# Denominators' epsilon on ScalarE, first loads interleaved, and new engine orders in a linear-attention and GEGLU block

## The chip, the cores and the metric

The kernel runs on one core of a Trainium2 chip. The metric is the device time of one execution in microseconds; the time before is the median of six runs. One further thing is read: one profiled execution, whose trace gives every instruction's start and length on each engine.

## The reference

A transformer block on x of 2048 rows and 448 columns, in bf16: layer norm, linear attention with 16 heads of 28, a residual; layer norm, a gated GELU feed-forward of width 1792, a residual.

```python
q, k, v = qkv[0], qkv[1], qkv[2]
phi = lambda t: jnp.where(t > 0, t + 1, jnp.exp(t)) + 1e-6
pq, pk = phi(q), phi(k)
kv = jnp.einsum("bhsd,bhse->bhde", pk, v)
z = jnp.einsum("bhsd->bhd", pk)
num = jnp.einsum("bhqd,bhde->bhqe", pq, kv)
den = jnp.einsum("bhqd,bhd->bhq", pq, z)[..., None] + 1e-6
o = num / den                     # then @ wo, and h = x + o @ wo
h2 = h + (gelu(hn @ w_gate) * (hn @ w_up)) @ w_down      # hn = layernorm(h)
```

## The kernel before

The rows are 16 tiles of 128. Every piece of work is a named task on one engine, written with what it reads and writes; the engines' orders are five lists of task numbers (`ORDERS`), and each engine runs its list strictly in order, waiting on semaphores where a task's inputs come from elsewhere. So an instruction that waits holds up everything behind it in its list. The number after the underscore is a tile, or a job of the feed-forward.

Stage A, for each tile t: `bnst1_t` and `bnag1_t` on VectorE (statistics, L347 and L348), `ln1_t` and `rstd1_t` on ScalarE (L354, L356: the reciprocal root as exp of -0.5 log). Tiles 0 to 3 are normalised on VectorE (`normD_t`, L369), transposed on TensorE (`tr0_t`, `tr1_t`, L377) and copied out by ScalarE and VectorE (`evxA_t`, `evxD_t`). Tiles 4 to 15 are normalised on GpSimd (`normP_t`, L387) and transposed by DMA from SP's queue (`xT_t`, L389), which stands behind all the first loads. Then TensorE projects `k_t` and `q_t` (L403), four matmuls each; ScalarE and VectorE make phi(k) (`ek_t`, `ck_t`, `pk_t`), and TensorE sums pk against the normalised x and a column of ones into four PSUM banks (`pt4_t`, L422; for the last tile `pt1_15` and `pt3_15`). Q is evacuated by ScalarE twice (`eq_t` exp, `rq_t` relu, L430 and L431) and joined on VectorE (`cq_t`, `aq_t`).

Between the stages the sums are brought to SBUF: `z1`, `z0` (the sum of phi(k), on all partitions), `evpA`, `evpD`; `kv` forms the heads' matrices (L461), `kvm` masks them to the heads' blocks on VectorE (L465), `w2_g` multiplies by Wo and `evwA`, `evwD` copy the result.

Stage B, for tiles in pairs: the product phi(q) z (`t1`, L487, on GpSimd but for tile 0), `dr_t` sums it per head (L490), `de_t` adds epsilon (L492), `rd_t` takes the reciprocal (L493), `pn_t` scales phi(q) by it (L494), all on VectorE. The pair is transposed, the first on TensorE (`tro`, copied by `evo`), the others by DMA (`oT_p`, L509). `out2_t` applies the w2 matrices (L522), `hr_t` adds x (L528), and the second layer norm follows: statistics on VectorE, the root on GpSimd (`negm2`, `vpe2`, `pow2`), `nhP_t` on GpSimd (L557), `wrap_t` on VectorE, `hT_t` a DMA transpose on SP (L560). The first pair goes through ScalarE, VectorE (`nhD_t`, `wr64_t`) and TensorE (`trh_t`, L549; `evhA_0`, `evhD_1`).

The feed-forward runs in chunks of 2, 2, 4, 4 and 4 tiles. A job is one bank of gate and one of up: `gu2_0` to `gu2_13` (28 matmuls of 256 columns) for the first four tiles, `gu4_14` to `gu4_55` (14 of 512) for the rest. Gate and up have two banks each; a job's halves go through ScalarE (`ge0_v`, `ge1_v`, gelu, L622) and VectorE (`hm0_v`, `hm1_v`, times up, L624), and the bank is free after that. `gu2_7` needs `hT_2` and `hT_3`; `gu4_14` needs `hT_4` to `hT_7`; `gu4_28` and `gu4_42` the next four each. `down448_t` multiplies by W_down (L574), `fo448_t` adds the residual (L578), `do_t` stores.

SP's queue carries, in order: the first loads (x tile by tile or in groups, Wk, Wq, Wv, Wo), the `xT` transposes, the gate and up weights, then `oT`, `hT` and stores as listed, with the load of W_down (`dwd`) among them. ScalarE's queue issues two loads at the start, the second of which (the last 64 rows of Wk) waits for a GpSimd memset, and only then its first table load.

Of the kernel before, what the change touches and what calls it, by code (L numbers as in the profile page):

```python
# [6 lines left out]
F32 = mybir.dt.float32  # L7
ALU = mybir.AluOpType
AF = mybir.ActivationFunctionType
# [6 lines left out]
    "28 34 36 45 43 65 75 70 78 52 54 63 61 91 81 69 130 86 74 85 101 113 90 125 105 140 117 152 129 164 144 156"  # L16
    " 176 168 188 203 193 215 180 227 192 242 207 219 231 246 247 257 248 251 288 232 260 292 290 294 296 254 263"
    " 312 269 314 316 317 272 275 266 353 330 334 431 436 441 446 451 456 384 461 503 508 415 466 469 513 518 523"
    " 528 533 575 580 585 590 487 541 595 600 605 610 615 620 625 630 635 640 559 538 672 648 703 645 654 651 719"
    " 724 729 734 739 744 749 754 759 764 769 774 779 784 801 806 811 816 821 826 831 836 841 846 851 856 861 866"  # L20
    " 789 792 795 798 871 874 877 880 883",
    "4 6 27 31 32 40 41 35 44 66 76 49 50 58 59 77 53 96 71 62 97 92 108 93 109 82 80 120 121 135 136 87 79 147 148"
    " 102 114 159 171 160 131 172 198 132 126 141 199 183 222 184 210 211 223 153 165 237 177 238 189 204 194 216"
    " 228 195 243 282 286 285 249 259 250 258 252 234 233 262 253 291 261 255 295 313 315 271 264 265 256 273 274"
    " 324 325 267 326 270 327 276 277 268 331 336 434 432 437 439 444 442 447 449 454 452 459 457 462 464 506 511"
    " 509 504 516 514 519 521 526 524 529 531 536 534 576 578 581 583 588 586 593 591 596 598 603 601 606 608 611"
    " 613 616 618 623 621 626 628 633 631 636 638 643 641 720 722 725 727 732 730 735 737 742 740 747 745 752 750"
    " 755 757 760 762 767 765 770 772 777 775 782 780 787 785 802 804 809 807 812 814 819 817 822 824 827 829 834"
    " 832 839 837 844 842 847 849 854 852 859 857 864 867 869 862",
    "29 30 38 39 33 42 37 46 47 56 48 67 57 94 51 95 60 68 55 106 64 107 133 118 72 119 73 134 83 145 84 157 88 146"  # L30
    " 196 208 89 158 169 103 170 104 115 197 181 116 209 220 127 221 182 128 142 143 339 154 155 300 298 166 235 167"
    " 236 340 178 179 190 301 191 337 205 299 338 217 206 218 229 230 369 244 370 245 284 283 302 287 304 305 308"
    " 306 289 343 402 344 347 309 293 310 307 345 311 346 348 297 349 350 375 318 376 321 319 400 377 320 322 546"
    " 323 403 328 371 332 333 329 372 357 335 401 379 354 358 355 380 359 435 433 381 378 438 356 440 382 445 443"
    " 544 406 448 407 450 364 474 367 410 472 411 408 412 547 453 455 460 409 458 659 475 413 473 657 463 465 385"
    " 388 386 482 389 483 512 387 484 390 688 416 507 419 505 417 420 660 418 478 421 395 398 510 554 690 555 470"
    " 556 517 479 515 426 691 520 429 522 545 527 525 667 485 530 532 480 550 537 535 481 668 658 577 579 551 669"
    " 582 584 467 589 557 663 587 664 689 552 491 553 492 594 592 488 489 694 597 599 490 698 604 602 493 695 607"
    " 609 612 614 696 699 501 617 619 700 701 624 622 670 627 629 498 665 634 632 666 639 637 697 644 542 560 563"
    " 561 642 564 565 562 539 673 676 573 674 675 570 649 704 677 705 678 707 646 706 708 709 721 723 714 683 652"  # L40
    " 726 728 717 733 731 736 738 686 743 741 748 746 655 753 751 756 758 761 763 768 766 771 773 778 776 783 781"
    " 788 786 803 805 810 808 813 815 820 818 823 825 828 830 835 833 840 838 845 843 848 850 855 853 860 858 868"
    " 790 793 863 870 796 865 799 872 875 878 881 884",
    "16 1 18 19 21 22 0 17 23 20 2 24 98 99 110 111 25 122 137 123 138 26 149 150 161 173 162 174 200 212 224 185"
    " 186 201 213 225 239 240 303 341 342 373 374 405 404 361 362 360 366 363 477 549 391 392 393 476 394 397 423"
    " 424 422 662 428 425 548 661 693 692 494 495 496 500 497 567 566 568 572 569 680 679 711 681 710 712 682 716"
    " 713 685",
    "3 5 7 8 9 10 11 12 13 14 15 100 112 124 139 151 163 175 187 202 214 226 241 278 279 280 281 351 352 383 365"
    " 368 414 396 471 399 427 430 486 468 558 671 702 499 502 540 543 574 571 647 718 687 653 684 656 715 650 791"
    " 797 800 873 794 879 876 882 885",  # L50
# [120 lines left out]
def bass_sequential_preLN__linear_attn_block__glu_gated_geglu__prompt_kernel(  # L171
# [14 lines left out]
    SEQ = "K0 K1 Q0 Q1 K2 K3 Q2 K4 K5 K6 Q3 K7 K8 K9 K10 K11 Q4 K12 K13 K14 Q5 K15 Q6 Q7 Q8 Q9 Q10 Q11 Q12 Q13 Q14 Q15"  # L186

    G = _Graph()
    es = ExitStack()
    with es:  # L190
        block = es.enter_context(nc.Block())

        def sb(name, shape, dt):
            return es.enter_context(nc.sbuf_tensor(name, shape, dt))
# [37 lines left out]
        den = sb("den", [128, 4, H, 2], F32)  # L232
# [11 lines left out]
        def bufs(name, n):  # L244
            return [_Buf("%s%d" % (name, i)) for i in range(n)]
# [8 lines left out]
            _Buf(n) for n in ("ident", "ones", "mones", "mtmp", "mask", "eps", "mhalf", "powtmp"))  # L254
        b_st1, b_mv1, b_nm1, b_ln1, b_rs1 = bufs("st1", T), bufs("mv1", T), bufs("nm1", T), bufs("ln1", T), bufs("rs1", T)
# [25 lines left out]
        def dma(q, out_ap, in_ap, w, name, r=(), after=()):  # L281
            t_ = G.add(q, lambda e: e.dma_start(out_ap, in_ap), r=r, w=w, name=name, kind="dma", after=list(after) + last[q])
            last[q] = [t_]
            return t_
# [11 lines left out]
        def dma_x(q, a, b):  # L296
            dma(q, x_sb[:, a:b, :], xv[:, a:b, :], b_x[a:b], "dx%d" % a)
# [4 lines left out]
        dma_x("act", 1, 2)  # L302
        dma_w3("sp", wk_sb, D, b_wk, "dwk")
        tk = dma_w1("act", wk_sb, D, b_wk, "dwk_t")
        dma_w3("sp", wq_sb, 0, b_wq, "dwq")
        dma_w1("sp", wq_sb, 0, b_wq, "dwq_t")
        dma_x("sp", 2, 4)
# [10 lines left out]
        op("pool", lambda e: e.memset(eps_t[:], EPS_LN), [], [b_eps], "eps")  # L318
        op("pool", lambda e: e.memset(mhalf[:], -0.5), [], [b_mhalf], "mhalf")
# [10 lines left out]
        tbl1 = G.add("act", lambda e: e.preload_act_table_set("natural_log_exp_and_others"), name="tbl1", kind="nosync", after=[tk])  # L330
# [147 lines left out]
        def a2_pair(p):  # L478
# [9 lines left out]
            for t in (a, a + 1):  # L488
                n, i = t % 2, t % 4
                op("dve", lambda e, n=n, i=i: e.tensor_reduce(den[:, i, :, 0], t1[:, n, :].rearrange("p (h d) -> p h d", h=H), AX.X, ALU.add),  # L490
                   [b_t1[n]], [b_den[i]], "dr_%d" % t)
                op("dve", lambda e, i=i: e.tensor_scalar(den[:, i, :, 0], den[:, i, :, 0], EPS, None, ALU.add), [b_den[i]], [b_den[i]], "de_%d" % t)  # L492
                op("dve", lambda e, i=i: e.reciprocal(rd[:, i, :], den[:, i, :, 0]), [b_den[i]], [b_rd[i]], "rd_%d" % t)  # L493
# [196 lines left out]
```

## Time and profile before

| what | value |
|---|---|
| median of six runs | 199.15 us (198.57 to 199.94) |
| the profiled execution | 199.94 us |
| its span, first to last instruction | 198.2 us |
| TensorE busy | 187.9 us |
| VectorE busy | 135.8 us |
| ScalarE busy | 74.6 us |
| GpSimd busy | 49.8 us |
| mean granted TensorE clock | 1.0 |

The profiled execution is the slowest of the six runs, 0.79 us above the median; 1.7 us of it lie outside the span. Matmul ends are modelled, so the length of a stage on TensorE is read from the starts of its tasks. "PEld" is TensorE's weight load, which overlaps matmuls.

### The profile page before, as it was taken

How to read it: one execution, taken by the hardware profiler on the slowest of the kernel's cores; microseconds unless marked ns; L12 is line 12 of the kernel's file. 1: busy time of each engine (PE TensorE's matmuls, PEld its weight loads, DVE VectorE, ACT ScalarE, POOL GpSimd, SP SyncE). 2: the span in 40 equal slices, each digit the busy share in tenths (PEclk: the TensorE clock that was granted, in tenths of full speed). 3: DMA queues.
4: the chain of work that ended last, by engine and by line, in shares of the span. 5: the costliest groups of instructions: out<-in, count | busy, mean ns of one | idle time of the engine just before them, and what ended most of it. 6: DMA issues, size and time to landing. Idle time of an engine off the chain costs nothing.

```text
span 198.2 us, 4143 instructions
## 1 busy us (share of the span) xinstructions
PE 187.9 (95%) x1572; PEld 114.0 (58%) x1572; DVE 135.8 (69%) x371; ACT 74.6 (38%) x210; POOL 49.8 (25%) x92
## 2 busy tenths in 40 slices
PE   7998999998899699979999999999999999999994
PEld 7444555644577565854445555545677777645553
DVE  3899978899899989687967787607645544424221
ACT  3795745698933120324133410013344344310000
POOL 6065640440353257513223013370000000000000
PEclk9999999999999999999999999999999999999999
DMA  6994448997907701623200187202630000000112
GB/s 182 370 171 81 91 97 170 222 219 130 315 4 83 120 3 22 139 50 76 46 11 0 24 134 154 55 0 50 134 74 3 0 0 3 0 10 16 46 46 73
DMA packets 35812, 16.98 MB, mean 86 GB/s; under 512 B 27728, under 2 KB 34512, under 8 KB 35792
## 3 DMA queue, kind: packets, MB, share of 16 engines
q1 hardware_dynamic: 35568, 16.55, 37.9%
q8 instruction: 12, 0.20, 0.5%
q10 hardware_dynamic: 224, 0.17, 0.3%
q14 instruction: 8, 0.07, 0.1%
HBM read 8.26 MB, written 1.84 MB: 51 GB/s over the span
## 4 chain that ended last, share of the span: by engine, by line
PE 75%; DVE 12%; DMA 8%; ACT 2%; issue 1%; ACTq 0%; DVEq 0%
PE ps L602 24%; PE ps L574 21%; PE ps L604 13%; PE ps L403 7%; DMA hnT<-hn 5%; PE ps L422 5%; PE ps L522 4%; DMA xnT<-xnn 2%; DVE den L490 2%; DVE den L492 1%; DMA x_sb<-in_A_x_dram 1%; DVE st L347 1%; DVE hh L624 1%; DVE pqn L494 1%; DVE x_sb L528 1%
## 5 line engine op out<-in xcount | busy, mean ns | idle before, releaser
L602 PE MATMUL ps<-hnT,wgu_sb 64*128 64x512 bf16 (+1 forms) x490 | 86.5, 333 | 3.6 <-DMA hnT<-hn 2.9
L604 PE MATMUL ps<-hnT,wgu_sb 64*128 64x512 bf16 (+1 forms) x490 | 86.7, 334 | 0.6 <-DVE hh L624 0.5
L622 ACT ACTIVATE gl<-ps 128x256 bf16<-128x256 f32 x112 | 36.9, 381 | 83.9 <-PE ps L604 76.2
L624 DVE TENSOR_TENSOR hh<-ps,gl 128x256 bf16<-128x256 f32 x112 | 42.8, 417 | 34.0 <-ACT gl L622 33.8
L602 PEld LDWEIGHTS ps<-hnT,wgu_sb 64*128 64x128 bf16 x490 | 45.2, 94 | 20.1 <-ACT gl L622 3.4
L604 PEld LDWEIGHTS ps<-hnT,wgu_sb 64*128 64x128 bf16 x490 | 42.5, 94 | 11.5 <-DVE hh L624 6.5
L574 PE MATMUL ps<-wd_sb,hh 128*128 128x448 bf16 (+1 forms) x238 | 43.4, 341 | 0.0
L574 PEld LDWEIGHTS ps<-wd_sb,hh 128*128 128x128 bf16 x238 | 23.1, 98 | 19.6 <-issue 0.4
L487 POOL TENSOR_TENSOR t<-pq,zbc 128x448 f32<-128x448 bf16 x15 | 16.2, 1090 | 38.7 <-DVE pq L483 25.3
L347 DVE BATCH_NORM_STATS2 st<-x_sb 128x6 f32<-128x448 bf16 x32 | 19.0, 608 | 3.8 <-DMA x_sb<-in_A_x_dram 3.7
L578 DVE TENSOR_TENSOR x_sb<-ps,x_sb 128x448 bf16<-128x448 f32 (+1 forms) x17 | 10.1, 592 | 15.2 <-PE ps L574 15.1
L403 PE MATMUL ps<-wk_sb,xnT 128*128 128x448 bf16 x64 | 14.4, 352 | 0.7 <-DMA xnT<-xnn 0.7
L522 PE MATMUL ps<-w,pqnT 112*128 112x448 bf16 x64 | 13.6, 353 | 0.6 <-DVE mv L348 0.6
L422 PE MATMUL ps<-pk,xnn 128*128 128x448 bf16 x64 | 14.0, 353 | 0.0
L403 PE MATMUL ps<-wq_sb,xnT 128*128 128x448 bf16 x64 | 13.8, 353 | 0.0
L528 DVE TENSOR_TENSOR x_sb<-ps,x_sb 128x448 bf16<-128x448 f32 x16 | 9.6, 615 | 2.3 <-PE ps L522 2.3
L414 ACT ACTIVATE e<-ps 128x448 bf16<-128x448 f32 x16 | 8.7, 544 | 6.3 <-PE ps L403 5.6
L387 POOL TENSOR_SCALAR xnn<-x_sb,nm,rs 128x448 bf16<-128x448 bf16 x12 | 8.8, 736 | 5.6 <-PE ps L422 2.9
L557 POOL TENSOR_SCALAR hn<-x_sb,nm,rs 128x448 bf16<-128x448 bf16 x14 | 10.0, 725 | 0.3
L416 DVE SCALAR_TENSOR_TENSOR pk<-ps,e 128x448 bf16<-128x448 f32 x16 | 9.7, 614 | 0.3 <-DVE e L415 0.2
L403 PEld LDWEIGHTS ps<-wk_sb,xnT 128*128 128x128 bf16 x64 | 6.1, 98 | 6.7 <-ACT rs L356 1.1
L522 PEld LDWEIGHTS ps<-w,pqnT 112*128 112x128 bf16 x64 | 5.7, 97 | 7.3 <-issue 1.3
(67 smaller groups left out, 141.8 us busy)
## 6 DMA issues: line engine op xcount, KB each, us to landing
out_dram<-x_sb SPq DMA_DIRECT2D x15, 112.0 KB, 1.7
wd_sb<-in_B_w_down_dram SPq DMA_DIRECT2D x1, 1568.0 KB, 7.6
x_sb<-in_A_x_dram SPq DMA_DIRECT2D x3, 448.0 KB, 5.4
wgu_sb<-in_B_w_gate_dram SPq DMA_DIRECT2D x1, 896.0 KB, 13.0
wgu_sb<-in_B_w_up_dram SPq DMA_DIRECT2D x1, 896.0 KB, 16.0
wgu_sb<-in_B_w_gate_dram SPq DMA_DIRECT2D x1, 672.0 KB, 5.9
wgu_sb<-in_B_w_up_dram SPq DMA_DIRECT2D x1, 672.0 KB, 8.4
wo_sb<-in_A_wo_dram SPq DMA_DIRECT2D x1, 392.0 KB, 7.3
```

Of the source, the lines that this page charges most:

```text
L347: op("dve", lambda e: e.bn_stats(st[:, t, :], src_ap), [b_src], [b_st[t]], "bnst%s_%d" % (tag, t))
L403: ins = e.matmul(ps[:, bk, 0:D], xnT[:, t, k, :], w[:, k, :], start=(k == 0), stop=(k == 3))
L422: ins = e.matmul(ps[:, BK_PT[c], 0:D], xnn[:, t % XN_R, c * 128:(c + 1) * 128], pk[:, i, :], start=(t == 0), stop=(t == T - 1))
L487: op(eng, lambda e, t=t, n=n: e.tensor_tensor(t1[:, n, :], pq[:, t, :], zbc[:, :], ALU.mult), [b_pq[t]] + b_z, [b_t1[n]], "t1%s_%d" % (eng ...
L522: ins = e.matmul(ps[:, BK_OUT[n], 0:D], pqnT[0:GW, i2, n, g, :], w2[:, g, :], start=(g == 0), stop=(g == NG - 1))
L528: op("dve", lambda e, t=t, bo=bo: e.tensor_tensor(x_sb[:, t, :], ps[:, bo, 0:D], x_sb[:, t, :], ALU.add), [b_ps[bo], b_x[t]], [b_x[t]], "h ...
L574: ins = e.matmul(psO, hh[:, j, (t % HR) * 128:(t % HR + 1) * 128], wd_sb[:, j, c0:c1], start=(j == 0), stop=(j == NJ - 1))
L578: op("dve", lambda e, t=t, psO=psO, c0=c0, c1=c1: e.tensor_tensor(x_sb[:, t, c0:c1], psO, x_sb[:, t, c0:c1], ALU.add), [b_ps[bk], b_x[t]], ...
L602: e.matmul(psG[:, jj * N:(jj + 1) * N], wgu_sb[A_, k, j * 128:(j + 1) * 128], hnT[A_, ka_, c0:c0 + N], start=(k == 0), stop=(k == NK - 1))
L604: ins = e.matmul(psU[:, jj * N:(jj + 1) * N], wgu_sb[B_, k, j * 128:(j + 1) * 128], hnT[B_, kb_, c0:c0 + N], start=(k == 0), stop=(k == NK ...
L622: G.add("act", lambda e, gi=gi, cs_=cs_, psG=psG: e.activation(gl[:, gi, cs_], psG[:, cs_], AF.Gelu_apprx_tanh), r=[b_ps[BK_G[i]]], w=[b_g ...
L624: op("dve", lambda e, dst=dst, srcU=srcU, srcL=srcL: e.tensor_tensor(dst, srcU, srcL, ALU.mult), [b_ps[BK_U[i]], b_glh], [b_ar[j_][t % HR] ...
```

## The change

Three things change. The add of epsilon to the denominators is a ScalarE instruction (an Identity activation whose bias is a column `eps_d`, which GpSimd fills), and `den` loses its unused second column. At the start tile 2 of x is loaded ahead of Wq and tile 3 behind it, and the last 64 rows of Wk are issued by SP behind the rest of Wk, not by ScalarE. The five orders and the order of K and Q (`SEQ`) are new: an order was searched with a model in which DMA transposes take time to issue.

```diff
-    SEQ = "K0 K1 Q0 Q1 K2 K3 Q2 K4 K5 K6 Q3 K7 K8 K9 K10 K11 Q4 K12 K13 K14 Q5 K15 Q6 Q7 ..."
+    SEQ = "Q0 K0 K1 Q1 K2 Q2 K3 K4 K5 Q3 K6 K7 K8 K9 K10 K11 K12 K13 Q4 K14 Q5 K15 Q6 Q7 ..."
...
         dma_x("sp", 0, 1)
-        dma_x("act", 1, 2)
+        tx1 = dma_x("act", 1, 2)
         dma_w3("sp", wk_sb, D, b_wk, "dwk")
-        tk = dma_w1("act", wk_sb, D, b_wk, "dwk_t")
+        dma_w1("sp", wk_sb, D, b_wk, "dwk_t")
+        dma_x("sp", 2, 3)
         dma_w3("sp", wq_sb, 0, b_wq, "dwq")
         dma_w1("sp", wq_sb, 0, b_wq, "dwq_t")
-        dma_x("sp", 2, 4)
+        dma_x("sp", 3, 4)
...
+        op("pool", lambda e: e.memset(eps_d[:], EPS), [], [b_epsd], "epsd")
...
-        tbl1 = G.add("act", ..., name="tbl1", kind="nosync", after=[tk])
+        tbl1 = G.add("act", ..., name="tbl1", kind="nosync", after=[tx1])
...
-                op("dve", lambda e, i=i: e.tensor_scalar(den[:, i, :, 0], den[:, i, :, 0], EPS, None, ALU.add), [b_den[i]], [b_den[i]], "de_%d" % t)
-                op("dve", lambda e, i=i: e.reciprocal(rd[:, i, :], den[:, i, :, 0]), [b_den[i]], [b_rd[i]], "rd_%d" % t)
+                op("act", lambda e, i=i: e.activation(den[:, i, :], den[:, i, :], AF.Identity, bias=eps_d[:, 0:1]), [b_den[i], b_epsd], [b_den[i]], "deA_%d" % t)
+                op("dve", lambda e, i=i: e.reciprocal(rd[:, i, :], den[:, i, :]), [b_den[i]], [b_rd[i]], "rd_%d" % t)
```

TensorE's order around the two stages, before and after (the jobs in a row shortened to a range):

```
before: ... k_12 q_4 k_13 pt4_10 k_14 pt4_11 k_15 pt4_12 pt4_13 pt4_14 pt1_15 pt3_15 q_9 q_6 q_7 kv
        q_5 q_10 w2_1 w2_0 w2_2 w2_3 q_8 q_11 tro_0 q_13 tro_1 out1_0 out1_1 q_14 q_15 q_12
        out2_2 trh_0 trh_1 gu2_0-5 out2_4 gu2_6-8 out2_6 down_0 down_1 gu2_9-13 gu4_14-17 out2_8
        down_3 gu4_18-27 out2_10 down_2 out2_12 down_5 out2_14 down_4 down_7 down_6 gu4_28-55 ...
after:  ... k_12 k_13 q_4 k_14 q_5 k_15 pt4_11 pt4_12 pt4_13 pt4_14 pt1_15 pt3_15 q_7 q_6 kv
        q_8 w2_1 w2_0 q_11 w2_3 q_9 w2_2 tro_0 q_10 tro_1 out1_0 out1_1 q_15 q_12 q_13 q_14
        trh_0 trh_1 out2_2 gu2_0 gu2_1 out2_4 gu2_2-5 out2_6 gu2_6-12 down_1 down_0 out2_8 gu2_13
        gu4_14 gu4_15 down_2 out2_10 gu4_16-19 down_3 out2_12 gu4_20-27 out2_14 down_4 down_5
        down_6 gu4_28-43 down_7 down_8 down_9 down_10 gu4_44-55 ...
```

On VectorE the new order of the first tiles is: statistics of tiles 0 and 1 around `normD_0`, statistics of tile 2, `evxD_0`, `normD_1`, `normD_2`, `evxD_1`. On ScalarE `rstd1_4` stands behind `rq_2`, and the adds stand as `deA_0` to `deA_5` among the evacuations of Q, `deA_7` first behind the GELU table load, the other nine between gelu halves. On SP `dwd` stands behind `oT_1 oT_2 oT_3 hT_3 hT_2`, where it stood behind `oT_1`.

## The prediction

> **What bounds the kernel now.** The page's first part comes first: TensorE is busy for 95% of the span and has the same 1,572 matmuls in any order, so the change can only win or lose TensorE's idle time.
>
> ```profile
> span 198.2 us, 4143 instructions
> ## 1 busy us (share of the span) xinstructions
> PE 187.9 (95%) x1572; PEld 114.0 (58%) x1572; DVE 135.8 (69%) x371; ACT 74.6 (38%) x210; POOL 49.8 (25%) x92
> ```
>
> Then I cut the span where the kind of work changes (busy us of each engine per stretch):
>
> ```profile
> core 0: us, PE busy (x) PEld busy (x) DVE busy (x) ACT busy (x) POOL busy (x), PEclk, DMA share, GB/s
> 6.30:16.60 10.30, 9.57 (x55) 4.36 (x52) 9.81 (x29) 8.41 (x27) 4.66 (x11) 1.00 0.87 232
> 16.60:36.30 19.70, 19.67 (x104) 10.20 (x105) 16.50 (x48) 10.62 (x31) 7.37 (x15) 1.00 0.59 122
> 36.30:53.10 16.80, 15.00 (x105) 8.22 (x105) 16.13 (x45) 14.95 (x35) 5.60 (x5) 1.00 0.97 217
> 53.10:68.10 15.00, 13.03 (x204) 9.98 (x204) 14.54 (x43) 5.73 (x15) 6.40 (x8) 1.00 0.52 84
> 68.10:87.70 19.60, 18.17 (x232) 13.16 (x233) 17.36 (x49) 4.61 (x14) 9.36 (x14) 1.00 0.31 62
> 87.70:195.30 107.60, 107.53 (x830) 63.51 (x830) 58.73 (x154) 27.66 (x84) 13.22 (x23) 1.00 0.20 43
> ```
>
> The reader should see that after 87.7 us TensorE idles for 0.07 us: nothing can be won there. Between 36.3 and 87.7 us VectorE is busy for 48.0 of 51.4 us and TensorE idles for 5.2; there VectorE, and the round trips through it, set the pace. Then the waits (total, times, longest) and two pieces of the chain (start, length):
>
> ```profile
> PEld ps L604 <- DVE hh L624: 6.5, 27, 0.6
> PE ps L602 <- DMA hnT<-hn: 2.9, 2, 1.6
> ```
> ```profile
> 62.98 5.04 DMA hnT<-hn
> 83.16 4.43 DMA hnT<-hn
> ```
>
> The two largest holes are gu2_7 waiting for hT_3 (1.65 us before 68.15) and gu4_14 waiting for hT_7 (1.23 us before 87.73). Many small ones are gate/up jobs waiting until VectorE frees their bank.
>
> **The change, step by step.** I follow the new order engine by engine with durations of the trace, start to next start where instructions stand back to back: a projection 0.757, gu2 1.525, gu4 1.512, out2 1.51, down 2.655 us on TensorE; on VectorE bn_stats, dr, pn, hr 0.53, hm 0.34, aq 0.30, cq and wrap 0.18, rd 0.16; a DMA transpose 1.25 us to issue, 2.5 (xT) to 3.1 us (oT, hT) to land.
>
> *The add of epsilon.* Sixteen instructions leave VectorE, sixteen join ScalarE.
>
> ```profile
> L492 DVE TENSOR_SCALAR den<-den 128x16 f32<-128x16 f32 x16 | 5.0, 313 | 0.0
> L354 ACT ACTIVATE ln<-mv,eps_t 128x1 f32<-128x1 f32 x18 | 5.0, 288 | 2.6 <-DVE mv L348 2.5
> L356 ACT ACTIVATE rs<-ln 128x1 f32<-128x1 f32 x18 | 3.5, 199 | 0.3
> ```
> ```profile
> 39.77 2.10 POOL L487 TENSOR_TENSOR t<-pq,zbc 128x448 f32<-128x448 bf16 x2
> 40.87 1.03 DVE L492 TENSOR_SCALAR den<-den 128x16 f32<-128x16 f32 x1
> ```
>
> The median add took 168 ns; the mean is 313 because some lie under a GpSimd product of L487 and stretch, one to 1.03 us. VectorE is rid of 16 x 0.31 = 5.0 us of busy time, some 3 us of it in the 51 us where it paces. On ScalarE the nearest row is the Ln with a bias pointer: 0.29 us (the Exp without one 0.20), so 16 x 0.29 = 4.6 us. The Trainium skill speaks against this: "ScalarE: Activation LUTs", in its rules for kernel authors, sends an add to VectorE and budgets about 0.3 us for each ACTIVATE with a bias pointer. By that rule ScalarE pays 4.8 us to relieve VectorE of 16 x 0.17 = 2.7 at the undisturbed price, a loss. The rows let me choose the other way: the price on VectorE was 5.0, and ScalarE has room where ten of the adds go (5.73 of 15.0 and 4.61 of 19.6 us busy). The other six fall where it has 1.85 us free in 16.8 (14.95 busy); that cover is thin, and is the first rival. Each rd now waits for two hops: dr's end, then 0.05 + 0.29 + 0.05 us. Behind it on VectorE stand pn and the hm's, for which TensorE waits. In the new order 0.3 to 2 us of other VectorE work stands between most dr and their rd, so I cost the hop at nothing; uncovered it is up to 0.4 us x 12 tiles.
>
> *The front.* The last 64 rows of Wk move from ScalarE's queue to SP's, tile 2 of x goes ahead of Wq, tile 3 behind it: 13 loads on SP instead of 11, the same bytes. Wk landed at 4.68; the 56 KB behind it and the 112 KB of tile 2, at its 336 KB in 1.5 us, put tile 2 at about 5.45 (7.03 before), Wq at 7.0 (6.21). VectorE now runs tile 2's statistics ahead of evxD_0 and normD_1: evxD_0 ends at 6.5 instead of 6.2, k_0 starts at 6.1 instead of 6.3 and holds 0.2 inside, q_0 at 7.3. rstd1_4 stands behind rq_2 on ScalarE: 12.4 instead of 11.2. normP_4 and xT_4 follow at 12.45 and 13.2 (12.06 before), and xT_4, which took 4.43 us beside the loads, lands at 15.7 to 17.6; TensorE is through with pt4_2 at 15.9 and takes k_4 at about 16.6, as before (16.63). From there each k waits for neither its transpose nor its pk by more than 0.1: k_8 starts at 22.0 (21.93). The front is worth 0, from -0.7 to +0.9.
>
> *36 to 53 us.* Two Q tiles instead of one now stand before k_15, so pt3_15 ends at 37.1 (36.3), with one Q less to do later. kv needs pt_sb 2: 1.9 us after pt1_15's sums are in, 39.05 (0.45 idle). kvm ends at 40.75, w2_1 at once; pn_0 ends 43.2 (43.67), its two adds gone from VectorE's queue; tro_0 at 43.25 (43.72); out1_1 waits 0.55 for evo_1; trh_1 0.1 for wr64_1; out2_2 runs after trh_1 while evhD_1 works, which removes the two holes of 0.62 and 0.72. gu2_0 at 52.45 instead of 53.08, the same work done: 0.6 won.
>
> *53 to 68 us.* From evhD_1 (51.6) VectorE's queue sums to 5.0 us until hm0_0 and 11.6 until wrap_2 ends, 63.2; hT_2 is issued at 63.3 and lands at 66.2, 68.3 if as slow as hT_3 was. TensorE has out2_6 as extra work before gu2_7: 7 x 1.525 + 2 x 1.51 = 13.7, with 0.9 of waits for hm it is there at 67.05. gu2_7 at 67.2, with 1.51 us more done than before at 68.15: 2.45 ahead, 1.85 of it here.
>
> *68 to 88 us.* 7 gu2, down 1 and 0, out2_8: 17.5 us. VectorE's sum is 10.6 us from hm_4 (64.1) to hm_10 (74.7); gu2_9 to gu2_12 each come within 0.4 us after the hm that frees their bank. wrap_7 stands behind fo448_1 (80.0); hT_7 lands at 83.1, 84.7 if slow; gu4_14 is due at 84.85. Before, 87.73 with out2_8 still to do: 87.73 + 1.51 - 84.85 = 4.4 ahead.
>
> Wd's load (1,568 KB) moves on SP from behind oT_1 to behind hT_2, from 47.6 to 64.6; at 7.6 us it lands at 72.2, before down 1 at 76.5 and before hT_4 is issued at 72.3.
>
> *After 85 us* gu4_28 needs hT_11 (about 121) at 123.8, gu4_42 hT_12 (143) at 145: covered. The stage stays full, and its length carries over.
>
> **The sum.** 0 + 0.6 + 1.85 + 1.95 = 4.4 us. I take 1.0 off: my sums hold no stretching of cq, aq and wrap under GpSimd's products, which did cost aq_8 and aq_13 1.3 us beyond their usual time between 66 and 77 us, and the slack at gu2_9 to gu2_12 is under 0.4. That leaves 3.4. The profiled execution took 199.94 for a span of 198.2; it would be 196.5, and the median, 0.8 below it, 199.15 - 3.4 = 195.8.
>
> **Rivals.** *ScalarE becomes the bound from 36 to 53 us.* Six adds, 1.6 us, less one Q tile's two evacuations (0.9) that moved ahead, come on top of 14.95 of 16.8. Were every us of it on the path, gu2_0 would come 0.75 later instead of 0.6 earlier: 195.8 + 1.35 = 197.1. For it: those evacuations free TensorE's banks. Against: 1.85 us were free.
>
> *The hop eats the gain.* If twelve rd's stop VectorE for 0.28 us each, that is 3.4 us: 199.2, no change. Against it stands the work placed in between.
>
> *Slower: hT_2 goes down with Wd.* It is now issued right before the 1,568 KB on the same queue. If it lands with them at 72.2, gu2_7 is 5.0 us late: 195.8 + 5.0 = 200.8; it decides from a landing at about 70.6 on. For it: hT_3 and hT_7 took 5.0 and 4.4 us even without a load. Against: oT_1, issued right before the same load, took 3.2 us.
>
> **How the numbers follow.** The walk 0.62 (194.0 to 197.6), ScalarE bound 0.12, no gain 0.09, hT_2 late 0.15, anything unforeseen 0.02, which I count as slower. 0.5% is 1.0 us, about what a measurement tells here. Faster: 0.62 and 0.10 of the ScalarE case, 0.72; same: its other 0.02 and 0.08 of the no-gain case, 0.10; slower: 0.15, 0.02 and the last 0.01, 0.18. The low end is the full 4.4 and 0.9 from the front, 194.0 rounded up a little; the high end, 200.2, takes in the no-gain case and leaves out the late hT_2.
>
> **What would show it.** gu2_0 near 52.5, gu2_7 near 67 with out2_6 behind it, gu4_14 near 85 with four out2 behind it, and TensorE full from there; the 1.2 us waits for hnT gone; ScalarE's new row near 0.25 us. I am wrong if xT_4 lands after 17.5, if VectorE idles before L493 for ScalarE's adds, or if hT_2 takes over 4 us.

## The result and the profile after

The changed kernel takes 197.29 us in the median (196.71 to 199.44), the kernel before 199.35 in the same series (198.48 to 200.46). The ratio is 0.9911, 95% interval 0.9896 to 0.9925: 1.8 us won, where the forecast had 3.4. The side was right, the size about half. A second series gave 0.9928 (0.9889 to 0.9966). A ratio leaves out the slow executions, those over 1.5% above the fastest of their kernel; this touches three runs below: the loads undone (five of twelve left out), W_down early (three of eleven) and the orders alone (one of four).

The profiled execution of the changed kernel took 199.24 us for a span of 197.2, so it is 2 us above its own median; a second profile (the repeat, below) has a span of 196.3. Against the 198.2 of before the two traces show 1.0 and 1.9 us won, and I read both. The median span of the first series is 195.4 us, of the second 196.3: the first trace shows an execution slower than is usual, the repeat a usual one of the second series. First the page's busy times (us, share of the span, instructions):

```profile
span 197.2 us, 4160 instructions
## 1 busy us (share of the span) xinstructions
PE 189.8 (96%) x1572; PEld 104.7 (53%) x1572; DVE 132.5 (67%) x355; ACT 77.5 (39%) x226; POOL 51.5 (26%) x93
```

VectorE lost 16 instructions and 3.3 us, ScalarE gained 16 and 2.9. The stretches, cut where the kind of work changes:

```profile
core 0: us, PE busy (x) PEld busy (x) DVE busy (x) ACT busy (x) POOL busy (x), PEclk, DMA share, GB/s
6.30:16.60 10.30, 10.14 (x59) 4.99 (x60) 9.91 (x32) 8.57 (x28) 3.00 (x8) 1.00 0.80 241
16.60:39.00 22.40, 20.52 (x108) 10.28 (x107) 17.35 (x49) 11.72 (x35) 8.37 (x20) 1.00 0.66 112
39.00:54.50 15.50, 14.71 (x100) 7.38 (x98) 15.44 (x39) 13.46 (x34) 5.90 (x6) 1.00 0.75 152
54.50:70.00 15.50, 14.59 (x215) 10.68 (x216) 14.54 (x42) 7.12 (x20) 7.51 (x9) 1.00 0.43 73
70.00:87.90 17.90, 17.90 (x232) 13.16 (x234) 17.43 (x46) 5.45 (x18) 10.37 (x14) 1.00 0.69 151
87.90:194.80 106.90, 106.89 (x826) 53.73 (x822) 55.45 (x146) 28.98 (x90) 12.77 (x22) 1.00 0.20 41
```

The stretch before gu4_14 (70.0 to 87.9) is full now; it held 1.4 us of idle time before. But 16.6 to 39.0, which was full before (19.67 of 19.70), idles for 1.9 us. The waits (total, times, longest) and the chain (start, length) name it:

```profile
PE ps L407 <- DMA xnT<-xnn: 1.8, 1, 1.8
PEld ps L608 <- DVE hh L628: 4.8, 17, 0.4
ACT den L496 <- DVE den L494: 1.3, 1, 1.3
```
```profile
20.06 5.02 DMA xnT<-xnn
25.08 0.14 issue
25.21 0.92 PE ps L407 x4
```

One transpose in the middle of stage A, xT_9, took 5.02 us where its median fellow takes 2.5, and k_9 waited for it. The two 1.2 to 1.7 us waits for hnT of before are gone. ScalarE's new line waits 1.3 us once for its input, and no VectorE instruction is listed as waiting for it.

When the named tasks start (us), and where TensorE's last instruction ends. "Epsilon alone" and "epsilon, fewer warm-ups" are experiments told below.

| task | before | forecast | after | repeat | epsilon alone | epsilon, fewer warm-ups |
|---|---|---|---|---|---|---|
| k_4 | 16.63 | 16.6 | 16.19 | 16.37 | 16.67 | 16.16 |
| k_9 | 23.44 | - | 25.21 | 24.29 | 23.48 | 23.07 |
| kv | 38.57 | 39.05 | 40.75 | 39.83 | 38.61 | 38.63 |
| gu2_0 | 53.08 | 52.45 | 54.49 | 53.57 | 52.91 | 52.94 |
| gu2_7 | 68.15 | 67.2 | 69.96 | 69.03 | 65.98 | 65.45 |
| gu4_14 | 87.73 | 84.85 | 87.92 | 86.99 | 85.28 | 83.94 |
| TensorE ends | 195.25 | - | 194.79 | 193.85 | 193.06 | 191.98 |
| span | 198.2 | - | 197.2 | 196.3 | 195.5 | 194.4 |

By gu2_7 the changed orders have done one out2 more than before (out2_6), and by gu4_14 also one more (out2_8), 1.51 us in either row; the two epsilon columns keep the orders of before, so their rows compare with before directly.

### The profile page after: what moved, and what is told of

It reads as the page before. It is cut to its first block, busy times and chain, and to the rows that moved or that the text cites. A ratio compares the mean times of both kernels' runs of the same rounds, so it can differ in the third digit from the quotient of the medians.

```text
span 197.2 us, 4160 instructions
## 1 busy us (share of the span) xinstructions
PE 189.8 (96%) x1572; PEld 104.7 (53%) x1572; DVE 132.5 (67%) x355; ACT 77.5 (39%) x226; POOL 51.5 (26%) x93
## 4 chain that ended last, share of the span: by engine, by line
PE 76%; DVE 10%; DMA 3%; issue 1%; POOL 1%; DVEq 0%; POOLq 0%
PE ps L606 27%; PE ps L578 22%; PE ps L608 16%; PE ps L526 5%; PE ps L407 4%; PE ps L426 3%; DMA xnT<-xnn 3%; DVE pqn L498 2%; DVE den L494 2%; DVE x_sb L532 1%; DVE st L351 1%; DVE w L479 1%; DVE rd L497 1%; POOL xnn L391 0%; DVE t L491 0%
## 5 line engine op out<-in xcount | busy, mean ns | idle before, releaser
L628 DVE TENSOR_TENSOR hh<-ps,gl 128x256 bf16<-128x256 f32 x112 | 43.3, 415 | 34.9 <-ACT gl L626 34.6
L606 PEld LDWEIGHTS ps<-hnT,wgu_sb 64*128 64x128 bf16 x490 | 44.1, 94 | 21.9 <-issue 3.0
L608 PEld LDWEIGHTS ps<-hnT,wgu_sb 64*128 64x128 bf16 x490 | 42.6, 94 | 15.0 <-DVE hh L628 4.8
L491 POOL TENSOR_TENSOR t<-pq,zbc 128x448 f32<-128x448 bf16 x15 | 16.6, 1118 | 31.6 <-DVE pq L487 22.7
L561 POOL TENSOR_SCALAR hn<-x_sb,nm,rs 128x448 bf16<-128x448 bf16 x14 | 11.6, 832 | 3.2 <-DMA hnT<-hn 2.6
L498 DVE TENSOR_TENSOR pqn<-pq,rd 128x448 bf16<-128x448 bf16 x16 | 11.1, 708 | 0.0
```

The lines of the kernel that those rows point to most:

```text
L491: op(eng, lambda e, t=t, n=n: e.tensor_tensor(t1[:, n, :], pq[:, t, :], zbc[:, :], ALU.mult), [b_pq[t]] + b_z, [b_t1[n]], "t1%s_%d" % (eng ...
L498: op("dve", lambda e, t=t, n=n, i=i, i2=i2: e.tensor_tensor(pqn[:, i2, n, :, 0:GW].rearrange("p g (h d) -> p g h d", h=4), pq[:, t, :].rea ...
L606: e.matmul(psG[:, jj * N:(jj + 1) * N], wgu_sb[A_, k, j * 128:(j + 1) * 128], hnT[A_, ka_, c0:c0 + N], start=(k == 0), stop=(k == NK - 1))
L608: ins = e.matmul(psU[:, jj * N:(jj + 1) * N], wgu_sb[B_, k, j * 128:(j + 1) * 128], hnT[B_, kb_, c0:c0 + N], start=(k == 0), stop=(k == NK ...
L628: op("dve", lambda e, dst=dst, srcU=srcU, srcL=srcL: e.tensor_tensor(dst, srcU, srcL, ALU.mult), [b_ps[BK_U[i]], b_glh], [b_ar[j_][t % HR] ...
```

## The experiments

Theory 1: the gain is cut short because blocks of TensorE's instructions are fetched through the same DMA engines as the transposes, and a transpose in flight at that moment can take 3.5 to 5.3 us. Theory 2: the parts work against each other, so that one gives all of the gain and the others nothing. They can both hold; the runs tell what each is worth.

**The changed kernel once more**, for the spread of its front.

> The changed kernel once more, unaltered, to stand beside its variants on one chip. In its first profile one transpose, xT_9, took 5.0 us instead of 2.5 and TensorE lost 1.95 us at k_9; a 16 KB packet of instructions was moving at 21.8 us, in the middle of it. Theory 1 (packets of instructions that share the DMA engines delay the transposes): the ratio to the kernel before is again 0.990 +- 0.003, and in the profile every transpose that takes over 3.5 us has a packet of the queues 8 or 14 within its time, whichever they are this time; if xT_9 lands in 2.5 us the span is near 195.2. Theory 2 (the two hops of the epsilon, and the scaling of phi(q) stretched under GpSimd, hold TensorE): slow transposes fall without packets, and the span stays near 197 with or without xT_9.

Measured 0.9928 (0.9889 to 0.9966). Here the slow transpose is xT_6 (4.15 us) and k_6 waits 0.84 us; xT_9 took its usual time, and kv starts 0.92 us earlier than in the first profile. So one instruction stream gives fronts that differ by 0.9 us.

**The epsilon, taken out and put in alone.** The changed kernel with the add back on VectorE, each in front of its reciprocal, and the kernel before with the add on ScalarE and nothing else:

```diff
-op("act", lambda e, i=i: e.activation(den[:, i, :], den[:, i, :], AF.Identity, bias=eps_d[:, 0:1]), ..., "deA_%d" % t)
+op("dve", lambda e, i=i: e.tensor_scalar(den[:, i, :], den[:, i, :], EPS, None, ALU.add), ..., "de_%d" % t)
...
# and the reverse on the kernel before, deA_t in ScalarE's list at the first task that began after dr_t ended
```

> The changed kernel with the add of epsilon alone back on VectorE, each add right before its reciprocal. Theory 1 and the prediction's step (16 x 0.31 us of VectorE, three of them in the stretch that it paces): slower than the changed kernel by 0.5 to 2 us. Theory 2 (the hop through ScalarE costs): faster by 0.5 to 2 us. If the time is within 0.5 us, the epsilon is worth nothing either way and the whole gain is the orders' and the loads'.

> The kernel before with the epsilon alone moved to ScalarE, each add put where ScalarE's queue stood when the sum of the head was ready; orders and loads as before. The prediction's sum gave the adds about 3 us of VectorE between 36 and 88 us. Theory 1: those are mostly behind the two waits for hT_3 and hT_7, which transposes delayed by packets set, so 0 to 1 us faster than the kernel before. Theory 2: 0.5 to 2 us slower, by the hops and by gelu halves held up behind adds that wait.

Measured: without the epsilon edit the changed kernel is no faster than before, 1.0011 (0.9989 to 1.0034). The edit alone gives 0.9900 (0.9869 to 0.9931), the whole gain of the change and twice what had been expected of it at most. On the old orders it is worth 1.9 us (199.09 to 197.24); on the new 1.2 to 2.0, as 199.30 is set against the repeat's 198.11 of the same series or against 197.29. The line of the add, in the changed kernel, in the kernel with the epsilon alone, and back on VectorE (ns, min/median/max):

```profile
L496 ACT ACTIVATE den<-den,eps_d x16: 292/306/318, 41.3 to 102.5; 128x16 f32<-128x16 f32 x16
```
```profile
L495 ACT ACTIVATE den<-den,eps_d x16: 298/308/379, 38.9 to 99.5; 128x16 f32<-128x16 f32 x16
```
```profile
L496 DVE TENSOR_SCALAR den<-den x16: 110/162/860, 40.1 to 104.2; 128x16 f32<-128x16 f32 x16
```

An add costs ScalarE about 0.31 us against VectorE's median of 0.16, but VectorE's went up to 0.86 and stood in the queue that paces the kernel. On the new orders the gain can be placed: from kv to gu2_0 it is 15.09 us with the add on VectorE and 13.74 with it on ScalarE, in the repeat too. With the add on VectorE, the one of tile 1 lies under GpSimd's products, pn_0 stands behind it on VectorE, and TensorE waits for pn_0 (timeline, then the wait in this run and in the changed kernel):

```profile
42.17 2.15 POOL L491 TENSOR_TENSOR t<-pq,zbc 128x448 f32<-128x448 bf16 x2 [0.40 <-DVE den L494]
43.49 0.86 DVE L496 TENSOR_SCALAR den<-den 128x16 f32<-128x16 f32 x1
```
```profile
PE ps L507 <- DVE pqn L498: 1.1, 1, 1.1
```
```profile
PE ps L507 <- DVE pqn L498: 0.2, 1, 0.2
```

On the old orders it comes elsewhere. In the run with the epsilon alone, pn_0 starts 0.94 us earlier than before (42.17 for 43.11), wrap_2 0.94 earlier and hT_2 is issued 0.93 earlier. gu2_7 starts 2.17 earlier, more than that: hT_3 took 3.80 us there against 5.04, a share that belongs to theory 1.

**The orders alone, and the loads in and out.** The changed kernel with both other edits undone; the changed kernel with only its loads undone; the kernel before with only the new loads:

```diff
-        dma_w1("sp", wk_sb, D, b_wk, "dwk_t")
-        dma_x("sp", 2, 3)
+        tk = dma_w1("act", wk_sb, D, b_wk, "dwk_t")
...
-        dma_x("sp", 3, 4)
+        dma_x("sp", 2, 4)
...
# the loads undone; for the loads alone the reverse on the kernel before, its orders kept
```

> The changed kernel with both the epsilon and the first loads as before: only the five orders are new. The epsilon alone gave 1.85 us on the old orders and its undoing cost 1.83 on the new; the loads' undoing cost about 1.7 on the new orders. If the parts add up: 199.1 + 1.7 = 200.8, slower than the kernel before. Theory 3 (the new orders lose in the front what they win later, unless the loads go with them) expects that, with k_0 held for 2 us inside by evxD_0 behind tile 2's statistics. If the orders are a gain by themselves: 198 or less.

> The changed kernel with the first loads as they were: the last 64 rows of Wk on ScalarE's queue with the table load behind it, tiles 2 and 3 of x in one load behind Wq. The new order of VectorE puts tile 2's statistics ahead of evxD_0; with tile 2 landing near 7.0 instead of 6.05 us, k_0's second half starts near 8 instead of 7.1, and xT_4 is issued 0.7 to 1 us later. Theory 1: 0.3 to 1.2 us slower than the changed kernel, less what other collisions move. If the front is covered whatever the loads do: the same within 0.3 us.

> The kernel before with the new first loads alone (and with the GpSimd memset that the last rows of Wk wait for put second, as the new kernel has it). There normD_0 and normD_1 do not stand behind tile 2's statistics, so an earlier tile 2 shortens only the 0.4 us that bn_stats of tile 2 waited, and Wq lands 0.7 us later, before q_0 needs it or just after. Within 0.5 us of the kernel before. If the loads are a gain by themselves: 1 us or more faster, and the loads do not only mend what the new orders broke.

Measured: the orders alone are slower, 1.012 (1.0079 to 1.0162), 2.4 us; the median is 201.72 where the parts would add up to 200.8. With the old loads and the epsilon they come to 1.0001 (0.9967 to 1.0034), and to a median of 199.96 us over all twelve executions, where at most 1.2 us over the changed kernel had been expected. The new loads alone on the old orders are slower too, 1.0076 (1.0048 to 1.0104), 1.5 us, where no more than 0.5 had been expected. So the orders and the loads belong together, and the pair is worth nothing. The run of the orders alone shows why they need each other (timeline: start, length, and in brackets the idle time and what ended it):

```profile
6.23 0.54 PE L406 MATMUL ps<-wk_sb,xnT 128*128 128x448 bf16 x2 [0.45 <-ACT xnT L385]
8.08 0.55 PE L406 MATMUL ps<-wk_sb,xnT 128*128 128x448 bf16 x2 [1.31 <-DVE xnT L387]
```

VectorE's new order has tile 2's statistics ahead of evxD_0, the second half of tile 0's copy. With the old loads tile 2 is late, and k_0 stands half done for 1.31 us. In the other direction, the new loads on the old orders bring Wq at 7.02 instead of 6.21 for little in return; xT_4 lands at 17.13, with a packet at 14.46 inside it, and k_4 begins 0.64 us later than before. The granted clock adds to the first loss (stretches of the same run; the clock is the figure ahead of the DMA share):

```profile
core 0: us, PE busy (x) PEld busy (x) DVE busy (x) ACT busy (x) POOL busy (x), PEclk, DMA share, GB/s
7.00:8.00 1.00, 0.00 (x0) 0.00 (x0) 0.96 (x4) 0.12 (x1) 0.00 (x0) 1.00 1.05 387
9.00:10.00 1.00, 1.00 (x4) 0.36 (x3) 0.87 (x3) 0.49 (x2) 0.00 (x0) 0.50 1.01 374
13.00:14.00 1.00, 1.00 (x9) 0.47 (x6) 0.82 (x4) 0.94 (x3) 0.24 (x1) 1.00 0.03 11
```

After the empty microsecond TensorE runs at half its clock for 3.4 us, an estimated 1.7 us more at most. The trace with only the loads undone shows the same dip, and that run's twelve executions sort by their mean clock: the five at 1.0 or 0.999 take 197.42 to 199.43 us, the five at 0.991 take 199.57 to 201.26, the two at 0.983 take 202.36 and 202.88. So both losses are the hole and its after-effect together.

**Moving the packets.** The trace lists two queues for instructions, whose packets have 16 KB (queue 8, twelve in a run) and 8 KB (queue 14). These are their times beside the transposes that took over 3.45 us, up to 90 us, worked out from the traces' DMA records (issue to landing, us):

```text
            16 KB packets                      8 KB packets       slow transposes
before      13.4 41.3 54.7 62.6 72.3 85.2 ...  20.9 23.6 42.8 66.1  xT_4 12.1-16.5, xT_5 13.4-17.2, xT_10 21.7-25.2,
                                                                    hT_2 61.7-65.7, hT_3 63.0-68.0, hT_7 83.2-87.6
after       21.8 42.9 56.3 66.0 74.1 82.1 ...  22.5 32.7 45.3 68.4  xT_9 20.1-25.1, xT_10 21.9-25.6, oT_2 53.6-58.4,
                                                                    hT_2 65.8-69.9, hT_6 80.8-85.0
repeat      17.3 45.2 55.4 65.2 73.3 81.2 ...  23.5 31.7 44.3 67.5  xT_6 16.3-20.5, xT_7 17.6-21.1, oT_2 52.7-57.4,
                                                                    hT_2 64.9-68.9, hT_6 79.9-84.2
```

Each slow one has a packet moving in its time; for xT_7 of the repeat it is one that began 0.35 us before the issue and took 1.5. Counted over all fourteen traces of this case, whole kernels: of 275 transposes that no packet overlaps, none took over 3.45 us; of 127 that a 16 KB packet overlaps, 75 did; of 60 that only an 8 KB packet overlaps, 6 did. So every slow one meets a packet, but not every one that meets a packet is slow. That is agreement, not proof; so the packets are moved. The warm-up at the start is 40 matmuls of 128 columns, and fewer, longer ones take instructions away without taking away any of the kernel's work:

```diff
-    WARM = 40
+    WARM = 20        # 10 in the runs named so
...
-                ins = e.matmul(ps[:, 3, 0:128], ones_bf[:], ones_bf[:], start=True, stop=True)
+                ins = e.matmul(ps[:, 3, 0:256], ones_bf[:], ones_w[:], start=True, stop=True)   # 0:512 with 10
...
+        op("dve", lambda e: e.memset(ones_w[:], 1.0), [], [b_onesw], "onesw")
```

First the changed kernel with 20 and the kernel before with 10:

> The changed kernel with its 40 warm-up matmuls of 128 columns made 20 of 256 (the ones of the moving side are a new tile that VectorE fills first): the same busy time at the start, 40 PE instructions fewer, so that every 16 KB packet of PE's instructions comes later in the work, by 1.1 us in the gate/up jobs of 256 columns. Theory 1: the packet at 55.4 to 56.3 us moves to about 57 and misses oT_2, which lands in 3.1 instead of 4.75 us; out2_4 no longer waits 0.94; the one at 65.2 to 66.0 moves to about 66.7 and still meets hT_2. 0.5 to 1 us faster than the changed kernel. Theory 2: oT_2 is slow for another reason (Wg and Wu, the pair's own size) and stays at 4.75 us; no change.

> The kernel before with 10 warm-up matmuls of 512 columns for its 40 of 128: 60 PE instructions fewer, so the packets come 1.6 us later in the 256-column jobs. Theory 1: the packet at 85.2 us moves to about 86.8 and misses hT_7, which lands in 2.9 instead of 4.4 us, and gu4_14 waits 0.1 instead of 1.5: 1 to 1.5 us faster than the kernel before; hT_2 and hT_3 are still met, by the one at 62.6, now near 64.2. Theory 2: hT_7 stays at 4.4 us and the time at 199.1.

The DMA view of the stretch in which oT_2 is in flight: the busy share in tenths of 40 equal slices, and the issue with its us to landing. The changed kernel, 52.5 to 60:

```profile
DMA  0000000000005999999230000000000000000000
q8 instruction: 1, 0.02, 0.7%
pqnT<-pqn SPq DMA_TRANSPOSE x1, 4.8
```

and with 20 warm-ups, 52 to 59:

```profile
DMA  0000000000002999999810000000040000000000
q8 instruction: 1, 0.02, 1.1%
pqnT<-pqn SPq DMA_TRANSPOSE x1, 3.0
```

In the second the packet stands by itself, in the slice with the 4, after the transpose has landed, and oT_2 takes 3.05 us instead of 4.75; the 0.94 us that out2_4 waited are gone. (The changed kernel's wait list puts that wait down to VectorE's mv, but what out2_4 needs of VectorE, hr_2 and hr_3, had ended by 55.75; oT_2 landed 0.14 us before it began.) In the first it falls at 56.30 on the transpose's tail: the row goes to 0 there, yet oT_2 lands only at 58.36. The kernel before, 61.9 to 68.2, where hT_2 and hT_3 are in flight:

```profile
DMA  0000404999990000079999999994000001039999
q8 instruction: 1, 0.02, 1.2%
hnT<-hn SPq DMA_TRANSPOSE x2, 4.5
```

and with 10 warm-ups, 61.9 to 67:

```profile
DMA  0000000089999999502999999999200000000000
q8 instruction: 1, 0.02, 1.7%
hnT<-hn SPq DMA_TRANSPOSE x2, 3.1
```

Before, the engines move next to nothing for a time in the middle of the two, and the pair lands after 4.0 and 5.0 us. The packet now comes at 65.44, later than the 64.2 expected, when the second has nearly moved its data, and they take 2.98 and 3.28; they had been expected to stay slow. hT_7 goes from 4.43 to 2.97, xT_4 from 4.43 to 2.49. gu2_7's wait of 1.65 us is gone, and gu4_14 begins at 84.84 for 87.73.

The times: before with 10 warm-ups is 0.9919 (0.9889 to 0.9949), 1.6 us faster, although k_0 begins half a microsecond later. Besides the warm-up's own shape only the number of instructions that TensorE has fetched by then is changed, and the transposes that were slow no longer are; so these packets cost the kernel before about 1.6 us. The changed kernel with 20 is 0.9916 (0.9886 to 0.9945), the same as without, and misses the 0.5 to 1 us expected: oT_2 was mended, xT_9 (4.79 us) and hT_2 (4.17) were not.

Then the same with 10 warm-ups on the other kernels:

> The kernel before with the epsilon on ScalarE, and with 10 warm-up matmuls of 512 columns for its 40 of 128. There hT_7 took 4.5 us with a packet at 82.8 and gu4_14 waited 1.4 us. Theory 1: the packet comes near 84.4 and misses hT_7: 1 to 1.4 us faster than with the epsilon alone, about 196.0, below the changed kernel. Theory 2: 197.2, as with the epsilon alone.

> The changed kernel with 10 warm-up matmuls of 512 columns for its 40 of 128, 60 PE instructions fewer. Theory 1: with the first packet near 24 us it meets xT_11 or xT_12, whose k waits for them have 2 us of cover there, and not xT_6 or xT_9; the second of the feed-forward misses oT_2: 1 to 2.5 us faster than the changed kernel, 195 to 196.3. Theory 2: no change.

> The kernel before with the epsilon on ScalarE, the new first loads and 10 warm-up matmuls of 512 columns: everything but the new orders. If the loads are worth nothing on the old orders: 196.65, as without them. If they are a gain by themselves: 196 or less.

The epsilon alone with 10 warm-ups gives 0.9878 (0.9846 to 0.9910), 2.4 us, the lowest median measured, 196.65; the waits before gu2_7 and gu4_14 are gone. Over the epsilon alone that is 0.6 us by the medians of two series (197.24 and 196.65), less than the 1 to 1.4 expected, and the intervals overlap; they overlap with that of the changed kernel's 0.9911 too. The two edits do not add up: 1.0% and 0.8% give 1.2%. Both make hT_3 and hT_7 land earlier, the one by their issue and the other by moving the packets, so they buy partly the same microseconds; between the two runs with 10 warm-ups (197.59 and 196.65) the epsilon is worth about 0.9 us. With the new loads besides, it is again 0.9878 (0.9855 to 0.9901): the loads are worth nothing there either.

The changed kernel with 10 missed what was expected of it. Its trace is what theory 1 asks for: xT_9 at its usual time, oT_2 3.04, hT_2 2.90, TensorE done at 192.8, though xT_13 is now hit (4.02 us) and k_13, which I had held to be covered, waits 0.90. Its span is 195.3, 1.0 and 1.9 us under the two traces of the changed kernel, but its median is 197.8 and its ratio 0.9901 (0.9870 to 0.9932), not to be told from 0.9911. The two traces are no fair measure here, since the changed kernel's median span is 195.4 in the first series. Why mended transposes don't show in the median is open: packets may fall elsewhere in other executions, as they do between the two traces, but no run has a trace of each.

**W_down's load early again.** In the changed kernel its number on SP's list goes back behind oT_1, to test whether a late Wd holds hT_2.

```diff
-    ... 282 283 353 385 416 370 367 354 398 ...
+    ... 282 283 353 354 385 416 370 367 398 ...     # 354 is dwd
```

> The changed kernel with the load of Wd issued behind oT_1 again, as in the kernel before. The prediction's slower rival had hT_2 held by Wd issued behind it. If it is (hT_2 took 4.06 us in the changed kernel): hT_2 lands in 2.9 us and gu2_7's wait of 0.31 goes. Theory 1 (hT_2 meets the packets at 65 and 67 to 68 us): hT_2 stays at 4 us and the time within 0.5 us of the changed kernel; Wd then shares the queue with oT_2 at most.

Measured 1.0057 (1.0021 to 1.0093), 2.9 us slower than the changed kernel, where at most 0.5 had been expected. hT_2 took 4.17 us without the load behind it (packets at 68.94 and 71.34), and 2.90 in the run above with the load right behind it: the load does not hold it. What an early Wd does hold is oT_2 (the chain, a wait, and two stretches of this run):

```profile
53.01 6.54 DMA pqnT<-pqn
```
```profile
PE ps L526 <- DMA pqnT<-pqn: 2.6, 1, 2.6
```
```profile
58.00:59.00 1.00, 0.00 (x0) 0.00 (x0) 1.00 (x4) 0.44 (x2) 0.83 (x3) 1.00 0.00 0
62.00:63.00 1.00, 1.00 (x14) 0.70 (x12) 0.41 (x1) 0.00 (x0) 0.00 (x0) 0.50 0.87 160
```

The last fence has the columns of the stretches above. oT_2 lands after 6.54 us, out2_4 waits 2.6, and after those empty microseconds the granted clock is 0.50 until about 64. Here too the executions sort by their mean clock: four at 1.0 or 0.999 take 199.17 to 200.18 us, five at 0.991 take 201.30 to 202.45, two at 0.983 take 203.87 and 203.94. In these orders, putting Wd late is what makes room for oT_2, which I had not counted as a gain or a need.

## Why the prediction was right or wrong

Four things failed. The gain was read off an execution 0.79 us above the median and taken from the median in full. The last stage, said to carry over its length, grew by 0.86 us. The front, put at nothing, cost 1.70 and 0.78 us in the two traces. And the gain was put down to the new orders, where the runs give it to the epsilon.

*The sum by its own steps*, in us. "Late" is the measured start less the forecast one, in the first profile and in the repeat.

| step | forecast | late at its end | what happened |
|---|---|---|---|
| front, to kv | worth 0, range -0.7 to +0.9 | 1.70 / 0.78 | k_9 (1.95) or k_6 (0.84) held by a slow xT |
| 39 to gu2_0 | 0.6 won | 2.04 / 1.12 | 0.34 more lost; q_14 waits 0.47 for a bank that ScalarE empties, tro_1 0.35 for pn_1 |
| to gu2_7 | 1.85 won | 2.76 / 1.83 | 0.7 more: out2_4 behind oT_2, 4.75 us |
| to gu4_14 | 1.95 won | 3.07 / 2.14 | 0.3 more; hT_7 in time |
| after gu4_14 | "its length carries over" | 0.86 / 0.85 more | 106.87 us for the 106.01 of before without out2_8 |
| the tail | carries over | 0.49 / 0.49 less | 2.45 us for 2.94 |

4.4 less 3.07 and 0.86, plus 0.49, is the 1.0 of the first profile; 4.4 less 2.14 and 0.85, plus 0.49, the 1.9 of the second.

*From the trace to the median.* The forecast took the sum from the trace of before and then went 0.8 us lower, because that trace lay 0.8 above its median. The changed kernel's median span in the first series, 195.4, shows what became of this. The walk's 198.2 - 4.4 = 193.8, with what is alike in both traces put in (1.36 lost from kv to gu4_14, 0.86 after it, 0.49 got back), gives 195.5. So in a usual execution of that series the front costs about nothing, by this estimate; in the second series the repeat, with 0.78 at the front, is the usual one. Of the 1.5 us between the forecast 195.8 and the measured 197.29, some 0.8 is the step from trace to median, and 0.7 is what was lost beyond the 1.0 taken off. Where a usual execution of the kernel before is quicker than its trace is open; there is one trace of it.

*Right.* The side; that TensorE's idle time between 36 and 88 us is what can be won; that the two waits for hnT go; that the stage after gu4_14 stays full; that a deduction is due for what the walk leaves out. From kv to gu4_14 1.36 us of the 4.4 were not had, where I had taken 1.0 off. One of these stretches I had not named: my list of what lengthens under GpSimd's products had cq, aq and wrap. pn_1 went from 0.55 to 1.45 us under such a product, and tro_1 waits for it:

```profile
42.30 3.42 POOL L491 TENSOR_TENSOR t<-pq,zbc 128x448 f32<-128x448 bf16 x3
44.27 1.93 DVE L498 TENSOR_TENSOR pqn<-pq,rd 128x448 bf16<-128x448 bf16 x2
```

*Wrong, first: the front was "worth 0", and "from there each k waits for neither its transpose nor its pk by more than 0.1".* That failed in both traces, by 1.70 and 0.78 us at kv. I had given xT_4 room for a slow transpose "beside the loads" and every later xT 2.5 us. The transposes that took over 3.45 us aren't tied to the loads; every one of them meets a packet of instructions. In the changed kernel with the epsilon back on VectorE, whose TensorE stream and loads are the same, the packet fell at 13.66, no xT took over 3.5 us, and kv started at 39.18 against the forecast 39.05. So where no packet fell badly the walk to kv was good to 0.13 us, and what it lacked is this one resource. Once kv is late, everything behind it is: 1.70 of the 3.07 us at gu4_14.

*Wrong, second: "the stage stays full, and its length carries over".* It stays full, but it is 0.86 us longer than the same work was. The windows show TensorE busy all through, and the profile records no wait at these places: between gate/up and down or out jobs there are gaps of 0.14 to 0.31 us each (down_3 0.17, down_7 0.30, down_11 0.14, out2_14 0.31), and the new order leaves the gate/up jobs five times where the old one does three. The stage takes 106.86 to 107.08 us in all eight traces with the new orders. That the switches cost it is read off the traces; no run changes only them, and with the old orders too the stage grew, from 107.53 to 107.78 us, when the epsilon moved.

*Wrong, third: the credit.* My sum put 4.4 us down to the new order of work and let the epsilon appear as "its two adds gone". The runs turn that round: orders and loads together are worth 0 (1.0011), the epsilon 1.9 us. The trace with the epsilon back on VectorE shows how orders and loads come to nothing. They win 2.2 us from kv to gu4_14 (48.45 for 49.16, with one out2 more) and 0.5 in the tail, but kv is 0.6 later than before and the last stage 1.05 longer. That leaves 1.1 us between the two traces, and none between the medians: before's trace is 0.79 us above its median, this one 0.41 below. I had the right means of seeing it in the row with a mean of 313 ns for a median of 168, and the choice of that row against the rule of the Trainium skill ("ScalarE: Activation LUTs", an add belongs on VectorE) held: the add did cost more on ScalarE, 0.31 for my 0.29, and moving it won. But the sum never priced the edit by itself, on orders that stay as they were. It also read the row too low: of its 5.0 us, not 3 but 4.2 lie between 36 and 88 us (eleven adds).

*The rivals.* ScalarE as the bound from 36 to 53 us: 13.46 us busy of 15.5, 87% for 89% before, and of TensorE's waits there only q_14's 0.47 is for it; refuted as the bound. (Its working had six adds at 1.6 us; at the forecast's own 0.29 they are 1.74, and they took 0.29 to 0.31 each, more than the 0.25 of its signs. Of the ten adds said to fall where ScalarE is less busy, four run after 88 us.) The hop: no VectorE instruction waited for ScalarE's add; refuted. hT_2 held by Wd: hT_2 took 4.17 us with Wd early and 2.90 in a run with Wd right behind it; refuted. Its sign, that hT_2 "takes over 4 us", came true (4.06) for another reason. And the list of what would make me wrong had a line for a late xT_4, but none for a slow xT after the loads are done.

## What to carry to other kernels

When single DMA transposes of one kind take 4 to 5 us and their fellows 3, look for the packets of instructions among the DMA queues: an order that rests on a transpose landing with under 2 us of slack can be spoiled by them, and removing a few dozen instructions ahead of it moves them. What that wins depends on what they meet next: 1.6 us on the old orders here, nothing measurable on the new. Price each part of a change alone on the old orders before crediting the order that came with it: here 16 tiny adds taken off the pacing engine won all of it, although the median add costs more where it went. And give the mean of a row, not its median, to an instruction that stands beside another engine's long ones.

## What the runs showed of the hardware that was not expected

*Instructions compete with transposes.* Twelve 16 KB packets in 3,144 TensorE records (matmuls and weight loads) are one for every 262. The Trainium skill says so much in "Runtime: NRT & Kernel Launch", in its section on instruction fetch: blocks of 16 KiB or 256 instructions, brought by the sequencer's own DMA queue, and the cost of crossing a block mostly hidden. The traces agree with the first, and with the last for TensorE itself, which isn't seen to starve: after 87.7 us, where six of the packets fall, it idles for 0.07 us in the kernel before. But a transpose that meets a 16 KB packet took over 3.45 us in 75 of 127 cases, up to 5.3 us in the traces of before, after and the repeat, instead of 2.5 (xT) or about 3 (oT, hT), and in the kernel before that was worth about 1.6 us. When a packet comes isn't fixed by the program: in three executions of the same TensorE stream the first one fell at 13.66, 17.26 and 21.84 us, and kv followed at 39.18, 39.83 and 40.75. This may be part of why the changed kernel's runs spread over 2.7 us; no run tests that.

*The clock follows the idle share of a fixed stretch, not the length of a hole.* TensorE's granted clock went to 0.50 after a hole of 1.31 us (orders alone), 1.55 (loads undone) and 2.56 (W_down early), each time for 3.41 us. In the kernels before and after, holes of 1.65 and 1.78 us left it at 1.0. The clock records explain it. In every trace that has them the clock changes only after 3.41 us or a multiple (54.61, 136.53, 187.73, 191.15 and 194.56 us are 16, 40, 55, 56 and 57 times that; the end cuts the last record). These are the stretches just before the three falls, and the emptiest one that no fall followed, in the kernel before (columns as above; loads undone, orders alone, W_down early, before):

```profile
4.25:7.66 3.41, 1.63 (x18) 0.90 (x16) 1.27 (x4) 1.26 (x5) 0.00 (x0) 1.00 1.02 350
5.43:8.85 3.42, 1.66 (x14) 0.83 (x14) 1.62 (x6) 1.45 (x6) 0.00 (x0) 1.00 1.03 382
57.41:60.82 3.41, 1.14 (x7) 0.62 (x8) 2.88 (x11) 0.95 (x4) 2.64 (x4) 1.00 0.01 1
66.48:69.89 3.41, 1.76 (x34) 1.77 (x34) 3.41 (x8) 0.66 (x2) 0.67 (x1) 1.00 0.43 79
```

By its busy time TensorE is idle for 52%, 52%, 67% and 48% of them. In the ten traces with such records no stretch with less idle time was followed by 0.50, and every one with more was, at the end of the kernel too. So in these traces the line lies near one half. In the kernel before, where the wait for hT_3 falls, the stretch had an estimated 0.1 us less idle time than the least that was followed by a fall. The records begin at another time in each trace (4.25 to 7.56 us), so the same hole may be cut in two or not; that would explain why some executions of one kernel show the dip and others do not, but no run tests it.
